# Low parts of the split weights: a GpSimd subtract in SBUF in place of two matmuls and a PSUM copy

## The chip, the cores and the metric

The kernel runs on one core of a Trainium2 chip. A core has five engines that matter here: PE (TensorE, matmuls; PEld is its weight loading), DVE (VectorE), ACT (ScalarE), POOL (GpSimd) and SP (SyncE, which here only issues DMAs). The metric is the device time of one execution in microseconds (us), lower is better. Before the change it was 708.12 us in the median of 3 runs (707.08 to 708.73). One more execution was taken by the hardware profiler; all rows shown come from that one.

## The reference

For each of 4 batches and 8 heads a recurrence with a complex, elementwise decay runs over 768 tokens; its real part is read out by q. The result (3072 tokens x 384) goes through a gated feed-forward layer with weights of 384 x 1536, 384 x 1536 and 1536 x 384:

```python
for t in range(S):
    ar, ai = (a_re_n[:, :, t, :, None], a_im_n[:, :, t, :, None])
    new_re = ar * S_re - ai * S_im
    new_im = ar * S_im + ai * S_re
    kv = np.einsum('bhd,bhe->bhde', k[:, :, t], v[:, :, t])
    S_re, S_im = (new_re + kv, new_im)
    y[:, :, t] = np.einsum('bhd,bhde->bhe', q[:, :, t], S_re)
...
a = x @ w_a
b = x @ w_b
return (a * b @ w_out).astype(np.float32)
```

## The kernel before

**Units.** The work is cut into 12 units u (`NU`): two pairs of batches times six chunks of 128 tokens. Each unit passes through four steps.

- `prep(u)` (mostly DVE, some ACT) forms running products of the decay over the tokens of the chunk (lines 226 and 232 inside sub-blocks, 253 and 259 between them, 274 and 279 to join them), their inverse (282 to 305), and multiplies q and k by them (309 and 294). Line 294 is its last operation. `scale(u)` (177 to 192) works out the normalisation of the decay; that of unit u+1 is woven into `prep(u)`.
- `stack(u)` lays the scaled q and k out by heads with ten DMAs on SP's queue (line 331), from tile `qk` to tile `stk`. There is one `qk` and one `stk`, so the steps of neighbouring units follow each other through them.
- `attn(u)` (PE with DVE and ACT) makes scores from `stk` (364), masks them on DVE (367), transposes the keys (375, 379), multiplies by v and by the carried state (404), and updates the state (421 to 432). Its output is split into a high part `xh`, rounded to fp32r (408, ACT), and a low part `xl` (413, DVE).
- The feed-forward of the unit runs over 12 slices f of the hidden dimension. `gemm1` multiplies in three fp32r passes, high by high, high by low and low by high (465, 18 matmuls for a slice), then forms a*b and splits it again (473 to 476, ACT and DVE in turn). `gemm2` (483) does the same into the output, three slices later.

**Weights.** They arrive as float64 bit patterns: 36 tiles of 128 x 384 (12 slices f, three matrices m), loaded once, at the start. `split_weights` turns each into two fp32r tiles that stay in SBUF for the whole run. For each tile DVE builds the float32 number `t` from the bits with three operations (133, 135, 137); ACT rounds it to the high part `hi` (141); then the low part t - hi is made on PE: an fp32 matmul of `t` with the identity (146, shown as two instructions), plus an fp32r matmul of `hi` with the negative identity (147), both into one PSUM bank, and ACT copies the sum to `lo` (148). The PSUM tile is `ab` for f below 7 and `pm` from there on; these are also the tiles of `gemm1` and of the attention. The float32 `t` lives in tile `o_sb`, of which there are 3 buffers, shared with the output rows.

**Order.** The program text gives `scale(0)`, `prep(0)`, `stack(0)`, then the conversion of six slices, `attn(0)` interleaved with `prep(1)`, and then the loop over units. In unit 0 (w = 0) each slice f first converts one more slice of weights while there are any, `prep(1)` is drained by f = 4 and `stack(1)` issued, and `attn(1)` follows in pieces. The final order on each engine is drawn up when the program is built, by a planner that takes for each engine the earliest instruction in program order that its own cost estimates call ready (raised by `high_priority` for the attention's and the feed-forward's small operations). On the chip each engine then works through its queue in that fixed order. So conversions stand on DVE between the operations of `prep(0)`, where the planner saw gaps, and `attn(1)` ended up behind all of unit 0's feed-forward.

GpSimd does the mask, the identity and three `memset`s at the start (lines 89 to 110) and nothing later.

Of the kernel before, what the change touches and what calls it, by code (L numbers as in the profile page):

```python
# [8 lines left out]
F32 = mybir.dt.float32  # L9
# [5 lines left out]
ALU = mybir.AluOpType  # L15
# [31 lines left out]
CONV_ON_AB = 7  # L47
# [19 lines left out]
def tile_kernel(ctx: ExitStack, tc: tile.TileContext, a_d, qk_d, v_d, w_d, qn_d, kn_d, vn_d, an_d, out_d):  # L67
    nc = tc.nc
    vec, act, pe, sync = nc.vector, nc.scalar, nc.tensor, nc.sync
# [10 lines left out]
    ps_ab = fast.enter_context(tc.tile_pool(name="ps_ab", bufs=3, space=PSUM))  # L80
    ps_o = fast.enter_context(tc.tile_pool(name="ps_o", bufs=1, space=PSUM))
    ps_x = fast.enter_context(tc.tile_pool(name="ps_x", bufs=1, space=PSUM))
    ps_m = fast.enter_context(tc.tile_pool(name="ps_m", bufs=2, space=PSUM))


    ident = const.tile([128, 128], F32, name="ident")
# [26 lines left out]
    nident = const.tile([128, 128], F32, name="nident")  # L113
# [4 lines left out]
    def r(ap):  # L118
        return ap.bitcast(F32R)
# [7 lines left out]
    def split_weights():  # L127
        for f in range(NF):
            for m, (c0, n) in enumerate(WPART):
                raw = raws[f, m]  # L130
                t = moe.tile([128, n], F32, name="o_sb", bufs=O_BUFS)
                tu = t.bitcast(U32)
                vec.tensor_scalar(out=tu, in0=raw[:, :, 1], scalar1=3, scalar2=0x3FFFFFFF,
                                  op0=ALU.logical_shift_left, op1=ALU.bitwise_and)
                vec.scalar_tensor_tensor(out=tu, in0=raw[:, :, 0], scalar=29, in1=tu,
                                         op0=ALU.logical_shift_right, op1=ALU.bitwise_or)
                vec.scalar_tensor_tensor(out=tu, in0=raw[:, :, 1], scalar=0xC0000000, in1=tu,  # L137
                                         op0=ALU.bitwise_and, op1=ALU.bitwise_or)
                w_t[f, m] = wpool.tile([128, 2, n], F32, name=f"w{m}{f}")
                hi, lo = w_t[f, m][:, 0], w_t[f, m][:, 1]  # L140
                act.copy(out=r(hi), in_=t)
                if f < CONV_ON_AB:
                    lp = ps_ab.tile([128, 512], F32, name="ab")
                else:
                    lp = ps_m.tile([128, 512], F32, name="pm")
                pe.matmul(out=lp[:, 0:n], lhsT=ident, rhs=t, start=True, stop=False)  # L146
                pe.matmul(out=lp[:, 0:n], lhsT=r(nident), rhs=r(hi), start=False, stop=True)
                act.copy(out=r(lo), in_=lp[:, 0:n])
            yield


# [440 lines left out]
    def drain(gen, ns=None):  # L592
# [3 lines left out]
        for cost in gen:  # L596
            if left is not None:
                left -= cost or 0
                if left <= 0:
                    return  # L600

    ws = split_weights()
    drain(scale(0, a_tiles[0], z_first))
    drain(prep(0))
# [134 lines left out]
```

## Time and profile before

| quantity | value |
|---|---|
| runs, median (lowest to highest) | 708.12 us (707.08 to 708.73) |
| profiled execution, span from first to last instruction | 708.4 us |
| PE busy | 658.3 us, 93% |
| DVE busy | 565.0 us, 80% |
| ACT busy | 309.6 us, 44% |
| POOL busy | 5.6 us, 1% |
| mean granted TensorE clock | 0.977 |
| core's HBM traffic | 39.32 MB read, 4.72 MB written |

The span of the profiled execution lies inside the range of the three runs, so its microseconds can be set against their median as they are. Busy shares are averages over the whole span; the kernel has a start, in which the weights are converted and the first units are prepared, a long middle in which one unit follows another, and an end without `prep`. The prediction therefore reads the profile in stretches of time, and shows the rows it uses.

In a row of a group of instructions stand: line, engine, operation, tile written <- tiles read, shape, count | busy us, mean ns of one | idle time of the engine just before them and what ended it. In a row of the timeline: start, duration, engine, line, operation, and in brackets the idle time before it. In a row of stretches: busy us of each engine (instructions), granted TensorE clock, DMA share, GB/s.

### The profile page before, as it was taken

Reading aid. Unit: us, or ns where it says so; the run is one execution under the profiler, and the core shown is the slowest. Engines: PE = TensorE matmul, PEld = TensorE weight load, DVE = VectorE, ACT = ScalarE, POOL = GpSimd, SP = SyncE. Lnnn points to the kernel's source line nnn. Section 1 sums busy time; section 2 is a strip of 40 time slices with the busy share of each in tenths; the row PEclk is TensorE's granted clock in tenths of the full one; section 3 lists DMA queues with packets and bytes.
Section 4 is the critical chain, followed back from the end, with each engine's and each line's share of the span. In section 5 each row is a group of like instructions: output and inputs, shape, how many; then the busy total and the mean of one; then the engine's idle time right before and its main releaser. Section 6 shows DMA issues by size and latency. Waiting matters only on the chain.

```text
span 708.4 us, 14429 instructions
## 1 busy us (share of the span) xinstructions
PE 658.3 (93%) x5838; PEld 608.8 (86%) x5838; DVE 565.0 (80%) x1411; ACT 309.6 (44%) x618; POOL 5.6 (1%) x11
## 2 busy tenths in 40 slices
PE   3657899799999999999999999999999999999996
PEld 1224788689899899899899999999999999999995
DVE  5999799888888988888889989999899898332221
ACT  6347565524524624525446346254462424221221
POOL 3000000000000000000000000000000000000000
PEclk9985999989999999999999999999999999999999
DMA  8963300420511512413305125042160140400000
GB/s 316 402 246 90 119 1 1 146 87 1 158 52 41 162 31 68 134 31 106 111 16 157 60 69 149 27 133 74 34 198 2 40 148 12 110 23 2 23 1 28
DMA packets 30234, 63.95 MB, mean 90 GB/s; under 512 B 3664, under 2 KB 7248, under 8 KB 30160
## 3 DMA queue, kind: packets, MB, share of 16 engines
q1 hardware_dynamic: 26704, 58.23, 26.1%
q10 hardware_dynamic: 3456, 4.72, 1.9%
q8 instruction: 48, 0.79, 0.4%
q14 instruction: 26, 0.21, 0.1%
HBM read 39.32 MB, written 4.72 MB: 62 GB/s over the span
## 4 chain that ended last, share of the span: by engine, by line
PE 48%; DVE 37%; ACT 5%; DMA 5%; issue 2%; SPq 1%; DVEq 0%; ACTq 0%
PE ab L465 21%; PE o L483 10%; PE xp L404 6%; PE pm L364 4%; DVE qk L294 4%; DVE a_t L274 4%; DVE pr L226 4%; PE pm L421 3%; DMA stk<-qk 3%; DVE hl L476 3%; DVE h_t L474 3%; DVE z L232 2%; PE pm L375 2%; DVE z L279 2%; DVE pb L253 2%
## 5 line engine op out<-in xcount | busy, mean ns | idle before, releaser
L465 PE MATMUL ab<-xh,w 128*128 128x256 f32 x1728 | 334.5, 283 | 0.0
L465 PEld LDWEIGHTS ab<-xh,w 128*128 128x128 f32 x1728 | 275.5, 189 | 1.7 <-issue 1.0
L465 PE MATMUL ab<-xl,w 128*128 128x256 f32 x864 | 243.6, 282 | 0.0
L465 PEld LDWEIGHTS ab<-xl,w 128*128 128x128 f32 x864 | 162.5, 188 | 1.2 <-issue 0.8
L483 PE MATMUL o<-w,hh 128*128 128x384 f32 x576 | 151.3, 343 | 0.0
L473 ACT COPY h_t<-ab 128x256 f32<-128x256 f32 x144 | 53.3, 370 | 183.1 <-PE ab L465 183.0
L474 DVE TENSOR_TENSOR h_t<-ab,h_t 128x256 f32<-128x256 f32 x144 | 60.5, 420 | 62.2 <-ACT h_t L473 61.7
L483 PEld LDWEIGHTS o<-w,hh 128*128 128x128 f32 x576 | 96.2, 188 | 2.8 <-issue 2.8
L483 PE MATMUL o<-w,hl 128*128 128x384 f32 x288 | 97.3, 338 | 0.0
L475 ACT CAST hh<-h_t 128x256 fp32r<-128x256 f32 x144 | 58.0, 402 | 79.2 <-DVE h_t L474 78.8
L476 DVE TENSOR_TENSOR hl<-h_t,hh 128x256 fp32r<-128x256 f32 x144 | 60.4, 419 | 16.1 <-ACT hh L475 16.1
L364 PE MATMUL pm<-stk 128*128 128x128 f32 x384 | 60.7, 291 | 10.1 <-DMA stk<-qk 9.3
L226 DVE TENSOR_TENSOR pr<-z 128x192 f32<-128x192 f32 (+1 forms) x195 | 65.1, 340 | 5.4 <-ACT z L212 1.6
L364 PEld LDWEIGHTS pm<-stk 128*128 128x128 f32 x384 | 52.3, 199 | 16.4 <-issue 9.9
L146 PE MATMUL ab<-o_sb,ident 128*128 128x384 f32 x42 | 30.8, 835 | 27.8 <-DVE o_sb L137 27.8
L483 PEld LDWEIGHTS o<-w,hl 128*128 128x128 f32 x288 | 54.1, 188 | 0.1
L232 DVE TENSOR_TENSOR z<-pr 128x96 f32<-128x96 f32 (+1 forms) x195 | 47.1, 248 | 3.9
L404 PE MATMUL xp<-am,v_t 128*32 128x128 f32 x768 | 45.2, 283 | 2.7 <-DVE am L367 2.7
L274 DVE TENSOR_TENSOR a_t<-z,b_t 128x768 f32<-128x768 f32 x48 | 45.1, 951 | 0.0
L146 PEld LDWEIGHTS ab<-o_sb,ident 128*128 128x128 f32 x42 | 10.8, 298 | 37.8 <-DVE o_sb L137 27.3
L294 DVE TENSOR_TENSOR qk<-qk,z 128x1536 f32<-128x1536 f32 (+1 forms) x26 | 42.3, 1628 | 0.1
L367 DVE TENSOR_TENSOR am<-pm,mask 128x512 f32<-128x512 f32 x48 | 32.9, 685 | 6.0 <-PE pm L364 5.8
(98 smaller groups left out, 746.5 us busy)
## 6 DMA issues: line engine op xcount, KB each, us to landing
w<-in_dram SPq DMA_DIRECT2D x36, 384.0 KB, 8.0
qk<-in_dram SPq DMA_DIRECT2D x12, 768.0 KB, 4.8
stk<-qk SPq DMA_DIRECT2D x48, 192.0 KB, 3.3
a_t<-in_dram SPq DMA_DIRECT2D x11, 768.0 KB, 4.3
v_t<-in_dram SPq DMA_DIRECT2D x24, 256.0 KB, 2.6
stk<-qk SPq DMA_DIRECT2D x24, 192.8 KB, 3.3
out_dram<-o_sb ACTq DMA_DIRECT2D x24, 192.0 KB, 2.3
stk<-qk SPq DMA_DIRECT2D x16, 128.0 KB, 3.2
```

Source lines behind the costliest of these rows:

```text
L226: vec.tensor_tensor(out=pr[:, :, :, o:o + n], in0=view(zz, W + at_(i) + 2 * o, [[W, 2], [-W, 2], [2, n]]), in1=tok(slice(1, 3), i - 1, o, ...
L232: vec.tensor_tensor(out=tok(slice(1, 3), i, o, n), in0=pr[:, :, 0, o:o + n], in1=pr[:, :, 1, o:o + n], op=ALU.add)
L274: vec.tensor_tensor(out=pz[:, s].rearrange("p (j b e) -> p j b e", j=SUB // 2, e=2), in0=zb[:, 1 + s], in1=view(bb, (1 + k - s) * NB, [[0, ...
L294: vec.tensor_tensor(out=qk4[:, :, k, x0:x1], in0=qk4[:, :, 1, x0:x1], in1=z[:, k].rearrange("p (j t) -> p j t", j=NJ).unsqueeze(2).broadca ...
L364: pe.matmul(out=sp[:, h4], lhsT=stk[:, h, ks], rhs=stk[:, h, qs], start=True, stop=True)
L404: pe.matmul(out=xp[qd * 32:(qd + 1) * 32, ti], lhsT=l, rhs=rr, start=st, stop=sp_, tile_position=(0, qd * 32), skip_group_check=True)
L465: pe.matmul(out=ab[:, m * TOK:(m + 1) * TOK], lhsT=r(w_ab(f, part, m * NJ + i)), rhs=r(xt[:, i, :]), start=n == 0, stop=n == 8)
L473: act.copy(out=h_t, in_=ab[:, 0:TOK])
L474: vec.tensor_tensor(out=h_t, in0=ab[:, TOK:2 * TOK], in1=h_t, op=ALU.mult)
L475: act.copy(out=r(hh), in_=h_t)
L476: vec.tensor_tensor(out=r(hl), in0=h_t, in1=hh, op=ALU.subtract)
L483: pe.matmul(out=os_[tt][:, 0:DM], lhsT=r(ht[:, ts]), rhs=r(w_t[f, 2][:, part, :]), start=(f == 0 and n == 0), stop=(f == NF - 1 and n == 2))
```

## The change

In `split_weights` the PSUM tile, both matmuls and the ACT copy go. The low part is the difference of the same two SBUF tiles, `t` and `hi`, formed by one GpSimd `tensor_tensor` that writes `lo` as fp32r. DVE's three operations and ACT's rounding to `hi` stay. It does this for all 36 tiles.

```diff
                 hi, lo = w_t[f, m][:, 0], w_t[f, m][:, 1]
                 act.copy(out=r(hi), in_=t)
-                if f < CONV_ON_AB:
-                    lp = ps_ab.tile([128, 512], F32, name="ab")
-                else:
-                    lp = ps_m.tile([128, 512], F32, name="pm")
-                pe.matmul(out=lp[:, 0:n], lhsT=ident, rhs=t, start=True, stop=False)
-                pe.matmul(out=lp[:, 0:n], lhsT=r(nident), rhs=r(hi), start=False, stop=True)
-                act.copy(out=r(lo), in_=lp[:, 0:n])
+                nc.gpsimd.tensor_tensor(out=r(lo), in0=t, in1=hi, op=ALU.subtract)
```

## Prediction, made before the run

> **What bounds the kernel now.** I read the slices of the span first, since the edit touches only the weight conversion.
>
> ```profile
> PE 658.3 (93%) x5838; PEld 608.8 (86%) x5838; DVE 565.0 (80%) x1411; ACT 309.6 (44%) x618; POOL 5.6 (1%) x11
> ...
> PE   3657899799999999999999999999999999999996
> ...
> DVE  5999799888888988888889989999899898332221
> ```
>
> By the averages PE is the bound, and taking matmuls off it should pay. By the slices it is different at the start: PE runs at 3 to 7 tenths there and DVE at 9. Stretches of my own, cut where the chain of waits changes hands, say how long that lasts.
>
> ```profile
> core 0: us, PE busy (x) PEld busy (x) DVE busy (x) ACT busy (x) POOL busy (x), PEclk, DMA share, GB/s
> 8.50:61.20 52.70, 33.18 (x57) 14.92 (x57) 51.98 (x163) 26.69 (x53) 0.00 (x0) 0.87 0.74 288
> 61.20:84.00 22.80, 18.48 (x160) 14.81 (x161) 18.55 (x35) 13.90 (x26) 0.00 (x0) 0.78 0.49 151
> 84.00:133.00 49.00, 48.99 (x319) 43.72 (x319) 46.26 (x124) 29.14 (x64) 0.00 (x0) 1.00 0.07 22
> 133.00:157.00 24.00, 19.30 (x218) 15.41 (x217) 19.38 (x46) 11.07 (x17) 0.00 (x0) 0.86 0.43 128
> 157.00:708.00 551.00, 538.30 (x5091) 519.97 (x5090) 427.43 (x1037) 223.73 (x451) 0.00 (x0) 1.00 0.24 71
> ```
>
> From 8.5 us to 61.2 us DVE is busy for 51.98 of 52.70 us; that is `prep(0)` with conversions between its operations. Then comes `attn(0)`, and from 84 to 133 us both engines are full: PE with unit 0's feed-forward and the last conversions, DVE with `prep(1)`, conversions and the feed-forward's small operations. Which of the two decides is told by the chain of waits and by PE's timeline at the end of that stretch.
>
> ```profile
> 129.28 1.67 DVE qk L294
> 131.29 0.51 DVE qk L294
> 131.79 1.07 issue
> ...
> 135.68 4.23 DMA stk<-qk
> 139.95 0.81 PE pm L364 x2
> ```
>
> ```profile
> 134.14 0.34 PE L483 MATMUL o<-w,hl 128*128 128x384 f32 x1
> 136.40 1.01 PE L364 MATMUL pm<-stk 128*128 128x128 f32 x4 [1.92 <-DMA stk<-qk]
> ```
>
> PE ends unit 0's last `gemm2` at 134.48 us and has nothing left: unit 1's feed-forward needs `attn(1)`, which needs `stack(1)`, which needs line 294 of `prep(1)`, the last link on DVE. So up to 133 us DVE's queue sets the time, all 36 conversions included, and PE waits for it even now. After 157 us PE is busy for 538.30 of 551 us. A shift of the moment at which `attn(1)` can start is therefore handed on to the end almost whole, in either direction.
>
> **What is removed.** On PE, before 61.2 us the conversions run beside a saturated DVE and are worth nothing. In the feed-forward stretch there are 15 tiles (those on `pm`):
>
> ```profile
> 85.11 0.81 PE L146 MATMUL pm<-o_sb,ident 128*128 128x384 f32 x2
> 85.46 0.63 PE L147 MATMUL pm<-w,nident 128*128 128x384 f32 x1
> 85.93 0.81 PE L146 MATMUL pm<-o_sb,ident 128*128 128x384 f32 x2
> ```
>
> ```profile
> L147 PE MATMUL pm<-w,nident 128*128 128x384 f32 x15 | 8.0, 541 | 0.0
> L148 ACT CAST w<-ab 128x384 fp32r<-128x384 f32 x21 | 10.0, 477 | 18.3 <-PE ab L147 18.3
> L148 ACT CAST w<-pm 128x384 fp32r<-128x384 f32 x15 | 7.1, 478 | 3.0 <-PE pm L147 3.0
> ```
>
> From one tile's start to the next is 0.82 us, so 15 x 0.82 = 12.3 us of full-speed PE time goes. PE would finish unit 0 near 122 us instead of 134.5 and wait that much longer for `stk`, if DVE ends `prep(1)` when it does now. I count these 12.3 us at nothing; DVE is the cover, and it would have to finish 12 us sooner for all of them to count. ACT loses 10.0 + 7.1 = 17.1 us of copies; at 29.14 of 49 us it bounds no stretch, so that is nothing as well.
>
> What DVE itself can gain is idle time. It idles for 124.5 - (51.98 + 18.55 + 46.26) = 7.7 us between 8.5 and 133 us, and its longest waits are these:
>
> ```profile
> DVE h_t L474 <- ACT h_t L473: 1.6, 2, 0.9
> DVE pr L226 <- ACT z L212: 1.4, 2, 1.0
> DVE o_sb L133 <- DMA w<-in_dram: 1.4, 1, 1.4
> ...
> DVE o_sb L133 <- ACT w L141: 0.6, 1, 0.6
> ```
>
> The first shrinks when `gemm1` isn't delayed by conversions. The others stem from `prep`, a load and ACT; but three float32 tiles converted by 71 us now keep their `o_sb` buffers until PE reaches line 146 at 85.11, so the planner can move up to three tiles' DVE work into gaps between 71 and 85 us. I take -3 us for all of this (1.6 for the feed-forward's wait, the rest for the gaps), between 0 and -5.
>
> **What is added.** 36 subtracts on GpSimd. No row of before shows one. The nearest are its own operations at the start:
>
> ```profile
> L110 POOL MEMSET u<- 128x512 f32 x2 | 1.0, 520 | 0.1
> L90 POOL TENSOR_SCALAR_AFFINE_SELECT mask<-mask 128x128 f32<-128x128 f32 x1 | 0.3, 292 | 0.0
> L89 POOL MEMSET mask<- 128x128 f32 x1 | 0.2, 204 | 0.0
> ```
>
> The two sizes of `memset`, with no input, give (520 - 204) / 384 = 0.82 ns per element and 0.10 us fixed. The select reads one input: (292 - 99) / 128 = 1.51 ns per element, so an input adds 0.69. With two inputs that is 2.20 ns per element, and a 128 x 384 subtract takes 0.10 + 0.84 = 0.94 us. The lower bound is the memset's 0.42 us. The Trainium skill, "GPSIMD Engine Reference", section 3.1, gives 4497 ns for a two-input operation on 2048 elements; scaled to 384 that is an estimate of 0.84 us, which would make the sum below some 3 us smaller; no run so far shows one.
>
> As a queue, GpSimd carries this easily: nothing else is in it after 6.3 us, and 36 x 0.94 = 34 us lie in a stretch of 125. Behind a waiting subtract stand only later subtracts. Those who wait for it are `gemm1` and `gemm2` of its slice, and DVE's line 133 three tiles later, through the `o_sb` buffer. That loop is DVE 1.2 us, ACT 0.5 and GpSimd 0.94, near 2.7 us with three buffers, 0.9 us a tile; DVE needs 1.2 us of its own for one. Not a bound.
>
> What can cost is DVE itself. Its operations in these stretches, by kind:
>
> ```profile
> L135 DVE SCALAR_TENSOR_TENSOR o_sb<-w,o_sb 128x384 uint32<-128x384 uint32 x36 | 19.8, 552 | 0.1
> L137 DVE SCALAR_TENSOR_TENSOR o_sb<-w,o_sb 128x384 uint32<-128x384 uint32 x36 | 19.8, 552 | 0.1
> L133 DVE TENSOR_SCALAR o_sb<-w 128x384 uint32<-128x384 uint32 x36 | 12.7, 354 | 2.1 <-DMA w<-in_dram 1.4 <-ACT w L141 0.6
> ...
> L474 DVE TENSOR_TENSOR h_t<-ab,h_t 128x256 f32<-128x256 f32 x12 | 5.1, 421 | 1.6 <-ACT h_t L473 1.6
> ...
> L367 DVE TENSOR_TENSOR am<-pm,mask 128x512 f32<-128x512 f32 x4 | 2.8, 688 | 0.8 <-PE pm L364 0.8
> ...
> L413 DVE TENSOR_TENSOR xl<-xp,xh 128x384 fp32r<-128x384 f32 x2 | 1.1, 558 | 0.9 <-ACT xh L408 0.9
> ```
>
> Nearly all of DVE's work here reads two SBUF operands. For the same 384 elements line 133, with one operand, takes 354 ns and line 135, with two, 552 ns: supplying the second operand is what DVE's time goes into. A subtract on GpSimd reads two SBUF operands too. If both are served by the same reader, one stands while the other works. The trace has one overlap:
>
> ```profile
> 5.36 0.98 POOL L110 MEMSET u<- 128x512 f32 x2
> 5.49 0.56 DVE L178 SCALAR_TENSOR_TENSOR z<-z 128x384 f32<-128x384 f32 x1 [4.34 <-ACT z L177]
> ...
> 6.61 0.56 DVE L178 SCALAR_TENSOR_TENSOR z<-z 128x384 f32<-128x384 f32 x1 [0.57 <-ACT z L177]
> ```
>
> Line 178 takes 0.56 us beside GpSimd and 0.56 us without. But the memset reads nothing, so this excludes only a hold by writes. The price per subtract lies between 0 and 0.94 us of DVE time. I take a full hold whenever DVE is at a two-operand operation, because line 135 against 133 is the nearest row for what a second SBUF operand costs, and the memset row is of another kind. That share is 116.8 us busy, less 12.7 (133), 5.1 (474), 2.8 (367), 1.1 (413) and about 1.2 of small ones, so 93.9 of 124.5 us, or 0.75. The sum is 36 x 0.94 x 0.75 = +25.5 us.
>
> The Trainium skill, "SBUF — State Buffer" (its practical consequences of the port allocation), speaks against this change in so many words: DVE with two SBUF inputs and GpSimd reading SBUF share a read interface, and the later one fully blocks. By that rule the whole +25.5 us would be due; no run so far shows it.
>
> One more term is PE's clock.
>
> ```profile
> 64.00:66.00 2.00, 2.00 (x6) 1.24 (x5) 1.88 (x6) 1.24 (x3) 0.00 (x0) 0.50 0.81 233
> ...
> 68.00:70.00 2.00, 1.37 (x21) 0.98 (x20) 2.00 (x4) 1.48 (x4) 0.00 (x0) 1.00 0.73 197
> ```
>
> The granted clock is 0.50 as `attn(0)` starts and 1.00 from 68 us; the conversion matmuls keep PE busy just before. Without them `attn(0)` may run at 0.50 for some microseconds more. PE has gaps there, so I count 0, at most +3.
>
> **Sum.** 708.4 + 25.5 - 3 = 730.9, taken as 731 us. The span of 708.4 lies 0.3 us from the runs' median of 708.12, which changes nothing. With every subtract held against DVE whole (+33.8) and no gain it is 742; with no hold and the full -5 it is 703. A measurement of this kernel can tell about 0.2%, or 1.4 us, from no change.
>
> **Rivals.** *GpSimd works beside DVE.* If its reads do not stand in DVE's way, 708.4 - 3 gives 705 us, faster by 0.5%; the place is again the end of `prep(1)` on DVE. For it: GpSimd is idle, and the one overlap in the trace costs nothing. Against: that overlap reads nothing. It turns slower once a subtract costs DVE more than 3 / 36 = 0.08 us. Chance 0.17.
>
> *Half a hold.* If the operands interleave, or the planner puts many subtracts where DVE waits or reads PSUM, half of 25.5 less 3 gives +10, or 718 us. Chance 0.16.
>
> *PE's time counts.* If conversions on PE delay DVE through `h_t` more than I see, the 12.3 us come back: 696 us. For it: between 93 and 108 us the chain of waits runs over PE. Against: DVE still idles for only 2.7 us of the 49, so it cannot end much sooner. Chance 0.03.
>
> *More than a hold.* If writing fp32r or handing over between engines makes a subtract cost above 0.94 us, each 0.3 us more gives 36 x 0.3 x 0.75 = 8 us: 739 to 750. Chance 0.10.
>
> **How the numbers follow.** The forecast, a hold of some 0.5 to 0.9 us of DVE time per subtract, has 0.54; its own range is 722 to 742. Faster: 0.13 of the first rival's 0.17 and the 0.03, so 0.16. Within 0.2%: the rest of the first rival and an edge of the half hold, 0.05. Slower: 0.79. The range from 703 to 743 leaves out the 696 case and most of the last rival.
>
> **What would show it.** Right: POOL busy near 34 us in some 36 subtracts; DVE's line 135 and the scan operations at lines 226 and 232 longer in the mean, or gaps before them with a POOL releaser or none; the first line 364 after `stack(0)` later by 10 to 18 us than 64.8, `stack(1)` later by 20 or more than 133; PE idle long before `attn(1)`; from there on the stretches as long as now. Wrong: DVE's rows keep their durations (then 705), or `stack(1)` moves forward by more than 5 us.

## The result, and the profile after

| | median (lowest to highest), us | runs |
|---|---|---|
| before | 708.01 (707.08 to 708.73) | 4 |
| after | 732.35 (731.14 to 733.48) | 4 |

The change makes the kernel slower: ratio 1.034, 95% interval 1.0319 to 1.0361, +24.3 us. The profiled execution after has a span of 729.9 us and belongs to a run of 731.64 us. In the later runs, too, a span lies 1.7 to 2.1 us under its run's time, so the 708.4 us span of before belongs to an execution some 2 us above the median. The two traces therefore differ by 21.5 us where the medians differ by 24.3.

In the changed kernel every line behind 142 has a number lower by 6: 226 is 220, 259 is 253, 294 is 288, 331 is 325, 364 is 358, 474 is 468. Its page begins like this (engines, then the slices):

```profile
PE 615.1 (84%) x5730; PEld 589.9 (81%) x5730; DVE 590.5 (81%) x1411; ACT 295.7 (41%) x582; POOL 58.2 (8%) x47
...
PE   0000599719999999999999999999999999999997
...
DVE  6999889978898888888998989999899999323221
...
POOL 5344214300000000000000000000000000000000
```

PE has lost its 36 conversions (108 instructions) and does nothing in the first four slices. DVE has as many instructions as before (1411) and is busy for 25.5 us more. That is the whole result in one line: work that DVE was not given takes DVE time. The stretches, cut where those of before were cut (start, `stack(0)`, `stack(1)`, some 24 us later):

```profile
core 0: us, PE busy (x) PEld busy (x) DVE busy (x) ACT busy (x) POOL busy (x), PEclk, DMA share, GB/s
7.10:73.25 66.15, 0.00 (x0) 0.00 (x0) 65.68 (x163) 20.43 (x38) 29.05 (x19) 1.00 0.61 236
73.25:159.90 86.65, 61.04 (x432) 56.67 (x432) 77.62 (x160) 36.29 (x73) 23.57 (x18) 0.89 0.19 56
159.90:184.00 24.10, 19.49 (x223) 16.46 (x224) 21.32 (x55) 10.44 (x15) 0.00 (x0) 0.75 0.43 117
184.00:730.00 546.00, 534.58 (x5077) 516.80 (x5075) 424.61 (x1026) 224.87 (x451) 0.00 (x0) 1.00 0.24 72
```

Up to `stack(1)` the stretch was 124.5 us with DVE busy for 116.8 us; now it is 66.15 + 86.65 = 152.8 us with DVE busy for 65.68 + 77.62 = 143.3 us. So DVE's work grew by 26.5 us and its idle time from 7.7 to 9.5 us. The end of that stretch, in the chain of waits (start, us, engine, tile and line):

```profile
138.75 1.13 POOL w L142
139.93 1.86 PE ab L459 x7
141.79 5.13 PE o L477 x21
146.99 0.49 ACT o_sb L616
147.98 0.49 ACT o_sb L616
148.88 1.49 ACT a_t L276
...
158.09 1.77 DVE qk L288
159.88 0.59 SPq L325
...
162.63 3.09 DMA stk<-qk
165.77 0.81 PE pm L358 x2
```

`stack(1)`'s DMAs are issued at 159.88 us; on SP's timeline of before it was 132.98 us. That is 26.9 us later, 12.0 of it already at `stack(0)` (73.25 against 61.22). From there to the end after needs 570.0 us and before 575.4, so 5.4 us come back. 26.9 - 5.4 gives the 21.5 us between the spans. (Executions differ by a little here: e10 below, whose program up to unit 10 is that of before, issues `stack(1)` at 130.30 us. The shift is 27 to 30 us.)

How the hold looks in one place, on the timeline around 67 us:

```profile
66.23 1.10 POOL L142 TENSOR_TENSOR w<-o_sb,w 128x384 fp32r<-128x384 f32 x1 [1.04 <-ACT w L141]
66.40 1.34 DVE L137 SCALAR_TENSOR_TENSOR o_sb<-w,o_sb 128x384 uint32<-128x384 uint32 x1
67.67 0.94 DVE L299 SCALAR_TENSOR_TENSOR a_t<-a_t 128x768 f32<-128x768 f32 x1
...
68.36 1.10 POOL L142 TENSOR_TENSOR w<-o_sb,w 128x384 fp32r<-128x384 f32 x1 [1.04 <-ACT w L141]
68.53 1.14 DVE L133 TENSOR_SCALAR o_sb<-w 128x384 uint32<-128x384 uint32 x1
```

Line 137 took 0.55 us before and takes 1.34 here; line 133 took 0.35 and takes 1.14. Both carry the same 0.79 us more, whatever their own length. That reads as follows: the DVE instruction that comes up while a subtract runs stands until that has nearly ended, and then takes its usual time. It counts as busy meanwhile, so the hold shows in no list of waits. It shows when each DVE instruction is set against others of its line and shape (their lower quartile): up to `stack(1)` exactly 36 are longer by over 0.15 us, for 36 subtracts, 26 of them by 0.79 to 0.85 us, 26.2 us in all. The same comparison gives none for before. In the groups (up to 160 us):

```profile
L137 DVE SCALAR_TENSOR_TENSOR o_sb<-w,o_sb 128x384 uint32<-128x384 uint32 x36 | 22.1, 616 | 0.1
L135 DVE SCALAR_TENSOR_TENSOR o_sb<-w,o_sb 128x384 uint32<-128x384 uint32 x36 | 21.9, 612 | 0.1
L133 DVE TENSOR_SCALAR o_sb<-w 128x384 uint32<-128x384 uint32 x36 | 15.0, 422 | 0.0
L253 DVE TENSOR_TENSOR b_t<-pb 128x12 f32<-128x12 f32 x15 | 7.4, 496 | 0.0
L468 DVE TENSOR_TENSOR h_t<-ab,h_t 128x256 f32<-128x256 f32 x12 | 4.9, 412 | 0.0
L361 DVE TENSOR_TENSOR am<-pm,mask 128x512 f32<-128x512 f32 x4 | 2.8, 688 | 2.4 <-PE pm L358 2.4
```

Lines 135 and 137 rose from 552 ns, 133 from 354. Line 253, a tiny operation, went from 175 ns (line 259 before) to 496: six of its 15 were held. Lines 468 and 361, which read one of their operands from PSUM, stayed at their 421 and 688 ns. They ran beside a working subtract in four places only, and in none of them are they longer. One of the four:

```profile
123.74 1.43 POOL L142 TENSOR_TENSOR w<-o_sb,w 128x384 fp32r<-128x384 f32 x1 [2.01 <-ACT w L141]
123.75 0.55 DVE L135 SCALAR_TENSOR_TENSOR o_sb<-w,o_sb 128x384 uint32<-128x384 uint32 x1
...
124.22 0.41 DVE L468 TENSOR_TENSOR h_t<-ab,h_t 128x256 f32<-128x256 f32 x1
...
124.55 0.84 DVE L220 TENSOR_TENSOR pr<-z 128x192 f32<-128x192 f32 x1
```

Line 468 passes in its usual 0.41 us, and line 220 behind it (0.35 us by itself) carries what is left of the hold, 0.48 us.

### The profile page after: what moved, and what is told of

The parts are those of the page before. It is cut to its first block, busy times and chain, and to the rows that moved or that the text cites. A ratio compares the mean times of both kernels' runs of the same rounds, so it can differ in the third digit from the quotient of the medians.

```text
span 729.9 us, 14256 instructions
## 1 busy us (share of the span) xinstructions
PE 615.1 (84%) x5730; PEld 589.9 (81%) x5730; DVE 590.5 (81%) x1411; ACT 295.7 (41%) x582; POOL 58.2 (8%) x47
## 4 chain that ended last, share of the span: by engine, by line
PE 45%; DVE 41%; ACT 4%; issue 4%; DMA 3%; SPq 1%; POOL 0%; ACTq 0%; DVEq 0%; POOLq 0%
PE ab L459 20%; PE o L477 10%; PE xp L398 5%; DVE pr L220 5%; PE pm L358 5%; DVE a_t L268 4%; DVE qk L288 3%; DVE h_t L468 3%; DVE z L226 3%; DMA stk<-qk 3%; PE pm L415 3%; DVE hl L470 3%; DVE b_t L253 2%; DVE o_sb L135 2%; DVE pb L247 2%
## 5 line engine op out<-in xcount | busy, mean ns | idle before, releaser
L477 PE MATMUL o<-w,hh 128*128 128x384 f32 x576 | 153.0, 346 | 0.0
L358 PE MATMUL pm<-stk 128*128 128x128 f32 x384 | 64.2, 303 | 98.5 <-DMA stk<-qk 98.2
L358 PEld LDWEIGHTS pm<-stk 128*128 128x128 f32 x384 | 54.8, 207 | 104.6 <-issue 101.0
L477 PEld LDWEIGHTS o<-w,hh 128*128 128x128 f32 x576 | 97.8, 191 | 2.8 <-issue 2.6
L470 DVE TENSOR_TENSOR hl<-h_t,hh 128x256 fp32r<-128x256 f32 x144 | 62.0, 431 | 16.8 <-ACT hh L469 16.5
L220 DVE TENSOR_TENSOR pr<-z 128x192 f32<-128x192 f32 (+1 forms) x195 | 70.1, 366 | 4.7 <-ACT z L206 0.6
L142 POOL TENSOR_TENSOR w<-o_sb,w 128x384 fp32r<-128x384 f32 x36 | 52.6, 1470 | 82.0 <-ACT w L141 65.5
L141 ACT CAST w<-o_sb 128x384 fp32r<-128x384 f32 x36 | 18.3, 510 | 55.9 <-DVE o_sb L137 52.7
```

What stands on the lines that cost most here:

```text
L220: vec.tensor_tensor(out=pr[:, :, :, o:o + n], in0=view(zz, W + at_(i) + 2 * o, [[W, 2], [-W, 2], [2, n]]), in1=tok(slice(1, 3), i - 1, o, ...
L358: pe.matmul(out=sp[:, h4], lhsT=stk[:, h, ks], rhs=stk[:, h, qs], start=True, stop=True)
L470: vec.tensor_tensor(out=r(hl), in0=h_t, in1=hh, op=ALU.subtract)
L477: pe.matmul(out=os_[tt][:, 0:DM], lhsT=r(ht[:, ts]), rhs=r(w_t[f, 2][:, part, :]), start=(f == 0 and n == 0), stop=(f == NF - 1 and n == 2))
```

## The experiments

Each kernel ran on one chip beside the kernel before, and its ratio is against those runs. `stack(0)` and `stack(1)` are the times at which SP issues their DMAs, from each kernel's trace; "held" is the comparison just described, in instructions and us.

| kernel | median us | ratio to before, 95% | stack(0) | stack(1) | held |
|---|---|---|---|---|---|
| after | 732.35 | 1.034 (1.0319 to 1.0361) | 73.25 | 159.88 | 36, 26.2 us |
| e1_memset | 703.87 | 0.9945 (0.9923 to 0.9967) | 59.99 | 133.75 | 3, 0.9 us |
| e2_dve | 719.95 | 1.0175 (1.0158 to 1.0192) | 61.31 | 140.41 | none |
| e3_both | 738.86 | 1.045 (1.0424 to 1.0475) | 75.75 | 161.22 | 31, 23.4 us |
| e4_twice | 757.68 | 1.071 (1.0692 to 1.0729) | 89.05 | 184.31 | 69, 52.7 us |
| e5_copy | 713.20 | 1.0074 (1.0046 to 1.0103) | 65.40 | 139.38 | 27, 7.8 us |
| e6_late | 716.37 | 1.0117 (1.0088 to 1.0146) | 60.37 | 143.00 | 14, 10.0 us |
| e7_early | 724.44 | 1.022 (1.0188 to 1.0252) | 74.35 | 149.38 | 21, 16.1 us |
| e8_prio | 707.49 | 0.9993 (0.9975 to 1.001) | 60.52 | 131.87 | none |
| e10_tail | 707.22 | 0.9989 (0.9977 to 1.0001) | 59.75 | 130.30 | none |
| e11_act | 705.23 | 0.9964 (0.995 to 0.9978) | 59.94 | 131.02 | none |

The theory is the prediction's: GpSimd's reads of SBUF hold DVE. The rivals are that any occupied GpSimd does it, that the loss lies in the path of the low part (GpSimd's own length, buffers, order), or that the missing PE and ACT work plays a part.

**A GpSimd instruction that reads nothing.**

```diff
-                nc.gpsimd.tensor_tensor(out=r(lo), in0=t, in1=hi, op=ALU.subtract)
+                nc.gpsimd.memset(lo.bitcast(U32), 0)
```

> The subtract is replaced by a GpSimd memset of lo, which reads nothing; the low parts of the weights are left out (zero). If DVE lost its time to a hold by GpSimd's reads: DVE's rows keep their durations of before (line 135 at 0.55 us, 226 at 0.25), and with the matmuls and copies gone as in the change the time is 705 us (702 to 709). If the change lost its time to a new order of the planner, to buffers released later or to a cold PE clock: 720 to 732. If GpSimd's writes hold DVE as well: 718 to 725.

Groups of e1, up to 190 us:

```profile
L137 DVE SCALAR_TENSOR_TENSOR o_sb<-w,o_sb 128x384 uint32<-128x384 uint32 x36 | 19.8, 552 | 0.0
L135 DVE SCALAR_TENSOR_TENSOR o_sb<-w,o_sb 128x384 uint32<-128x384 uint32 x36 | 19.8, 552 | 0.1
...
L142 POOL MEMSET w<- 128x384 uint32 x36 | 15.1, 418 | 93.1 <-DVE o_sb L137 93.0
...
L133 DVE TENSOR_SCALAR o_sb<-w 128x384 uint32<-128x384 uint32 x36 | 13.5, 377 | 0.2 <-DMA w<-in_dram 0.2
```

36 GpSimd instructions in the same place of the program, and lines 135 and 137 keep their 552 ns to the nanosecond. The kernel is 4.0 us faster than before. An occupied GpSimd is thus hardly a cost; what a subtract adds to a memset is. One exception shows on e1's timeline:

```profile
100.36 0.42 POOL L142 MEMSET w<- 128x384 uint32 x1 [7.86 <-DVE o_sb L137]
100.38 0.61 DVE L133 TENSOR_SCALAR o_sb<-w 128x384 uint32<-128x384 uint32 x1
```

Three instructions of line 133, which has one operand, ran beside a whole memset (this one, and two at 8.87 and 83.83 us), and they are longer by 0.25 to 0.34 us. So a GpSimd instruction that only writes leaves the two-operand lines alone, but not line 133.

**One input, two inputs, two subtracts.** e5 puts a copy in the subtract's place, e4 issues the subtract twice:

```diff
-                nc.gpsimd.tensor_tensor(out=r(lo), in0=t, in1=hi, op=ALU.subtract)
+                nc.gpsimd.tensor_copy(out=r(lo), in_=t)
```

> GpSimd copies t into lo, one SBUF input in place of two (lo then holds t, so the difference is left out). If any GpSimd read holds DVE's two-operand instructions: a shorter hold, about 0.4 to 0.5 us each, 715 to 721 us, and single DVE rows longer by that much. If only an instruction with two inputs holds DVE: 703 to 706 us as with the memset.

> The change with every subtract done twice (same operands, same result). If each subtract holds DVE by about 0.70 us: another 25 us, 752 to 760 us. If the loss has another cause and GpSimd works beside DVE: 732 to 736 us.

The timeline of e5, a copy beside line 226:

```profile
29.03 0.64 POOL L142 CAST w<-o_sb 128x384 fp32r<-128x384 f32 x1 [2.61 <-DVE o_sb L137]
29.22 0.62 DVE L226 TENSOR_TENSOR z<-pr 128x48 f32<-128x48 f32 x2
...
30.37 0.32 DVE L226 TENSOR_TENSOR z<-pr 128x48 f32<-128x48 f32 x2
```

The copy costs DVE 0.62 - 0.32 = 0.30 us; of 27 held instructions 20 show 0.30 to 0.32. That is less than the 0.4 to 0.5 us expected, and so is the loss (713.20 us against 715 to 721). So on two-operand lines the hold grows with what GpSimd reads: none for the memset, 0.31 us for one input, 0.80 us for two. e4's groups, up to 190 us:

```profile
L142 POOL TENSOR_TENSOR w<-o_sb,w 128x384 fp32r<-128x384 f32 x36 | 45.3, 1258 | 68.9 <-ACT w L141 68.9
L143 POOL TENSOR_TENSOR w<-o_sb,w 128x384 fp32r<-128x384 f32 x36 | 43.9, 1221 | 2.7
```

72 subtracts hold 69 DVE instructions for 52.7 us, twice the 26.2, and the kernel is 25.3 us slower than after. Among the four kernels without PE's part and with GpSimd instead (e1, e5, after, e4) the time rises from 703.87 to 757.68 us while the held time rises from 0.9 to 52.7 us: 53.8 us for 51.8. DVE's hold is handed on almost one for one.

**The subtract on DVE itself.**

```diff
-                nc.gpsimd.tensor_tensor(out=r(lo), in0=t, in1=hi, op=ALU.subtract)
+                vec.tensor_tensor(out=r(lo), in0=t, in1=hi, op=ALU.subtract)
```

> The same subtract, done by DVE itself (36 x 0.47 us = 17 us more in its queue). If a GpSimd subtract costs DVE about 0.70 us each, doing it on DVE is cheaper: stack(1) 17 to 19 us later than before, 720 to 724 us in all. If GpSimd's subtract took little from DVE, this is the dearest version: 732 us or more.

The group of that line, up to 190 us:

```profile
L142 DVE TENSOR_TENSOR w<-o_sb,w 128x384 fp32r<-128x384 f32 x36 | 19.7, 552 | 0.0
```

DVE does the subtract in 0.55 us, and the kernel is 12.4 us faster than after. A subtract on GpSimd takes more of DVE's time (26.2 us for 36, 0.73 each) than the same subtract on DVE. There is a second effect: only 15 tiles stand ahead of `stack(0)` here and 2 behind `stack(1)`; before and after have 19 and none. `stack(0)` keeps its place (61.31 us), and `stack(1)` comes 7.4 us later than in before's trace, where 17 to 19 were expected. That reads as the planner reckoning with the price of a DVE instruction and spreading the work, while the hold is not in its costs: after's order has the tiles where before's has them.

**The subtract added to the kernel before.** e3 issues the subtract into `lo` and then lets PE and ACT write the same values as before:

```diff
                 act.copy(out=r(hi), in_=t)
+                nc.gpsimd.tensor_tensor(out=r(lo), in0=t, in1=hi, op=ALU.subtract)
```

> The kernel before with both matmuls and the PSUM copy kept, and the GpSimd subtract added in front of them (the copy then writes lo again). If the subtract alone costs the time: 729 to 735 us, as much as the change. If the removal of the matmuls costs it (PE clock, new order): 708 to 712 us. If the removal is worth its 12 us of PE time and the hold costs more than it seems: 740 us or more.

With PE and ACT doing all that they did, the time still rises, by 31.0 us: the loss does not come from what was taken away. That is between the two outcomes expected (729 to 735, and 740 or more). 23.4 us of it are held DVE instructions. Where the rest comes from isn't shown; one candidate is a wait that this edit makes itself, seen in e3's groups up to 190 us (the old ACT copy is its line 149):

```profile
L149 ACT CAST w<-ab 128x384 fp32r<-128x384 f32 x21 | 9.9, 477 | 27.7 <-PE ab L148 15.0 <-POOL w L142 12.7
```

**Half of the tiles.** e6 uses the subtract for f of 7 and up (15 tiles), e7 for f below 7 (21 tiles); the others go over PE and ACT:

```diff
                 act.copy(out=r(hi), in_=t)
+                if f >= CONV_ON_AB:
+                    nc.gpsimd.tensor_tensor(out=r(lo), in0=t, in1=hi, op=ALU.subtract)
+                    continue
```

> GpSimd subtracts the 15 tiles from f = 7 on; PE and ACT keep the first 21. If the hold is 0.70 us a tile and the removal is worth 4 to 6 us, all of it here where PE is full: 10.5 less 5, 711 to 716 us. If the late tiles cost nothing because PE is what counts there: 696 to 704 us.

> The other part: GpSimd subtracts the first 21 tiles, PE and ACT keep the last 15. The hold is 21 x 0.70 = 15 us and nothing is won on PE, which idles there: 720 to 726 us. If the early stretch has slack (loads, waits on ACT): 708 to 712 us.

Against the 708.65 us of before on the same chip they are 7.7 and 15.8 us slower, together 23.5, where the whole change is 24.3. Per tile that is 0.51 and 0.75 us. e7 lies in the range expected of a hold, e6 just above its own. Each half is worse than leaving its tiles on PE, so neither of the two divisions tried gains, and nothing in them points to one that would. In the 15 late tiles, which free 12 us of full-speed PE time, the loss is the smaller of the two, but it is a loss.

**Is PE's or ACT's part worth anything?** e8 leaves the computation as it was and raises the priority of the matmuls and the ACT copy:

```diff
+                with tc.high_priority(offset=MOE_FIRST):
                     pe.matmul(out=lp[:, 0:n], lhsT=ident, rhs=t, start=True, stop=False)
...
                     act.copy(out=r(lo), in_=lp[:, 0:n])
```

> The kernel before, with the two matmuls and the copy of each conversion raised in the planner's order, so that PE frees the float32 buffers earlier and DVE can convert in its gaps from 71 to 85 us. If the 4 us that the memset version gains come from those buffers and from the feed-forward's waits: 704 to 707 us. If they come from PE's or ACT's time itself: 707 to 709 us, no change.

e11 takes PE and GpSimd out altogether and lets ACT write `lo`:

```diff
-                nc.gpsimd.tensor_tensor(out=r(lo), in0=t, in1=hi, op=ALU.subtract)
+                act.copy(out=r(lo), in_=t)
```

> The matmuls go and neither GpSimd nor DVE gets the work: ACT copies t into lo (the difference is left out, lo holds t), one ACT copy a tile as before. If the 4 us of the memset version come from PE's 15 late tiles and the PSUM tiles they held: 703 to 705 us. If they come from ACT's 17 us: 707 to 709 us.

The priority changes nothing that can be measured (ratio 0.9993, interval 0.9975 to 1.001). Without PE's conversions and without a hold the kernel gains 2.9 us in e11 and 4.0 us in e1. That is about what all of PE's 36 conversions are worth. In e1 PE ends unit 0's last `gemm2` at 120.9 us instead of 134.5 and then stands; PE's waits between 60 and 170 us in e1:

```profile
PE pm L358 <- DMA stk<-qk: 80.2, 3, 63.5
```

63.5 us of that is the wait for `stack(0)` and most of the rest the one for `stack(1)`.

**GpSimd where DVE is not the bound.** Could a subtract on GpSimd pay elsewhere? e10 moves the feed-forward's split (line 476) of the last two units, where DVE's slices show two to three tenths, to GpSimd:

```diff
-    def gemm1(f, xh, xl, ps_ab=ps_ab, moe=moe):
+    def gemm1(f, xh, xl, ps_ab=ps_ab, moe=moe, sub=vec):
...
-            vec.tensor_tensor(out=r(hl), in0=h_t, in1=hh, op=ALU.subtract)
+            sub.tensor_tensor(out=r(hl), in0=h_t, in1=hh, op=ALU.subtract)
...
-            pend.append((w, f, *gemm1(f, *x_cur), os_))
+            pend.append((w, f, *gemm1(f, *x_cur, sub=nc.gpsimd if w >= NU - 2 else vec), os_))
```

> A control in the place where DVE does not decide: the kernel before, with the 24 low parts hl of the last two units (128 x 256 each) subtracted by GpSimd in place of DVE. If GpSimd's subtracts cost only through DVE's queue where that queue sets the time: 706.5 to 709.5 us, no change, with DVE rows held here as well. If a GpSimd subtract slows the kernel by itself (its latency, its port): 24 x 0.5 to 0.7, 718 us or more.

Its GpSimd group after 600 us, and one overlap on its timeline:

```profile
L476 POOL TENSOR_TENSOR hl<-h_t,hh 128x256 fp32r<-128x256 f32 x24 | 17.8, 743 | 672.6 <-ACT hh L475 672.6
```

```profile
640.72 0.69 DVE L367 TENSOR_TENSOR am<-pm,mask 128x512 f32<-128x512 f32 x1
...
641.23 0.74 POOL L476 TENSOR_TENSOR hl<-h_t,hh 128x256 fp32r<-128x256 f32 x1 [6.24 <-ACT hh L475]
```

Where a hold was expected here too, none came. That says little of the hold: DVE does nothing at all beside 20 of the 24 subtracts. The other four meet four instructions of line 367 and one of line 413, all with one operand in PSUM, and all five keep their usual length (0.69 and 0.56 us). The subtract is slower than DVE's 424 ns by 0.32 us, and the kernel comes out no different from before (0.9989, interval 0.9977 to 1.0001).

## Why the prediction was right

It said 731 us, by a hold of DVE; the median is 732.35 us, and the hold is what the runs show. The mechanism was right. That the number came out within 1.4 us is partly luck: two errors in the hold cancel, the gain of 3 us came from another place than the one named, and `stack(1)` moved by 27 to 30 us, more than the 22.5 of the sum, of which 5.4 came back. Step by step:

**DVE's queue up to `stack(1)` sets the time.** Right. Held DVE time is handed on nearly one for one (e1, e5, after, e4). That a shift of `stack(1)` reaches the end "almost whole" holds with a correction: 5.4 of 26.9 us came back. From `stack(1)` to the end after, e1, e4, e5 and e6 need 569.1 to 571.4 us, and before, e2, e3, e7, e8 and e11 need 572.3 to 575.5. One part of it can be seen: `stk`'s last transfer on the chain takes 3.09 us now and took 4.23 before, when unit 0's output left beside it. It is not PE's matmuls alone, since e11 has none either and needs 573.0. e6, which does without PE and ACT in the 15 late tiles alone, is in the first group, and e7, which keeps them there, is in the second. With e11, which keeps ACT's copies, that points to those copies; only e2 does not fit, and it converts two tiles behind `stack(1)`. Whether it is the ACT copies or the order in which units 1 and 2 are laid out stays open.

**The hold, 36 x 0.94 x 0.75 = 25.5 us.** The sum is right (26.2), and by luck, since its factors were wrong in opposite ways. One subtract, at 78.18 us, found no DVE instruction running: it takes 1.00 us, not 0.94, and holds DVE for 0.85. Each of the other 35 ends 0.85 to 0.88 us after a DVE instruction with all operands in SBUF that went ahead of it, and holds the next one mostly for 0.80. So part of a subtract's span is its own waiting, and the price per hit was below the 0.94. And the share is not 0.75: all 36 struck something. The share left line 133 out because it reads one operand; but it is held like the others (1.14 us against 0.35), as is line 231, another `tensor_scalar`. Only the operations with an operand in PSUM were right to leave out. Besides, a DVE that is at such an operation is soon at the next one. Now and then the hit is partial (ten of the 36 are under 0.79, four of them behind line 468 or 361), which makes the mean 0.73. The Trainium skill, "SBUF — State Buffer", section "Who interferes with whom", lists `tensor_scalar` among the operations that can take both ports and then contend with GpSimd; the trace agrees in that both lines are held, though it doesn't show which ports they used. The same section says that an operation with one SBUF input outside those modes doesn't contend, and that a GpSimd instruction which only writes doesn't disturb DVE's two inputs; lines 468 and 361 and e1's lines 135 and 137 agree. Its wording that the loser blocks for the whole instruction is a little more than the runs show: 0.85 of 1.00 us at 78.18.

The prediction took its full hold from lines 133 and 135: 354 against 552 ns for the same 384 elements, read as the price of a second SBUF operand. Before's groups don't bear that reading out. Line 226 takes 354 ns for 192 elements and line 135 552 for 384, both with two SBUF operands, which is 1.03 ns for each further element; line 367, with only one operand in SBUF, needs 688 ns for 512 and so the same. Line 133 is the one that differs: with 186 ns for the 48 elements of line 237 and 354 for its 384 a `tensor_scalar` takes 0.50 ns for each further element, twice the pace. The conclusion from the pair was right, the reason was not.

**POOL busy near 34 us.** Wrong: 52.6 us for the 36, 1470 ns each in the mean. The prediction had DVE held by GpSimd and not the reverse. On after's timeline:

```profile
55.57 1.81 DVE L268 TENSOR_TENSOR a_t<-z,b_t 128x768 f32<-128x768 f32 x2
...
56.27 5.31 POOL L142 TENSOR_TENSOR w<-o_sb,w 128x384 fp32r<-128x384 f32 x1 [3.49 <-ACT w L141]
57.31 0.95 DVE L288 TENSOR_TENSOR qk<-qk,z 128x768 f32<-128x768 f32 x1
...
59.05 0.35 DVE L133 TENSOR_SCALAR o_sb<-w 128x384 uint32<-128x384 uint32 x1
```

The subtract stands for 5.31 us behind a train of DVE operations without a gap. Being held is cheap for GpSimd, as the prediction's buffer loop has it, except at the very end (below).

**The gain of 3 us from DVE's idle time.** Right in size, wrong in place. Without a hold the removal gives 2.9 to 4.0 us (e11, e1); but DVE's idle time ahead of `stack(1)` did not shrink, it grew from 7.7 to 9.5 us. In e1 `stack(1)` comes 0.8 us later than in before's trace, so its gain lies wholly behind it. Why the idle grew is on the chain and on DVE's timeline:

```profile
146.97 0.93 DVE L273 TENSOR_TENSOR z<-a_t 128x768 f32<-128x768 f32 x1
...
148.88 1.48 ACT L276 ACTIVATE a_t<-z 128x1536 f32<-128x1536 f32 x1 [0.42 <-ACT o_sb L616]
150.39 0.96 DVE L282 TENSOR_TENSOR a_t<-a_t 128x768 f32<-128x768 f32 x1 [2.36 <-ACT a_t L276]
...
153.32 0.96 DVE L297 TENSOR_TENSOR a_t<-a_t 128x768 f32<-128x768 f32 x1 [1.97 <-ACT a_t L284]
```

DVE waits 2.36 and 1.97 us there; before it was 0.62 and 0.41 at the same operations. PE is done with unit 0 by 147 us, so no small feed-forward operations are left to fill DVE's pauses (before, lines 474 and 476 ran in them), and ACT reaches line 276 only behind the two output copies of line 616, which wait for the last `gemm2` and so for the last two subtracts.

**PE's 12.3 us and ACT's 17.1 us at nothing.** Nearly right: without PE's conversions e1 and e11 gain 2.9 to 4.0 us, and e1's PE finishes unit 0 early and then waits. The rival of 696 us is excluded; the best kernel without conversions is at 703.87.

**The span as the base.** The prediction set the span of 708.4 us against the median as if both measured the same. A run's time lies some 1.75 us above its span, so the base was an execution about 2 us slow. It moves the forecast by about 2 us, less than the terms above.

**PE's clock, 0 to +3 us, counted 0.** Right at `attn(0)`: between 76 and 96 us the granted clock is 1.00, against 0.50 and 0.55 before at the same work. It was not quite nothing at the end of unit 0. There PE waits for the last weights, and from 140 to 144 us the clock is 0.50, where before had 1.00 from 84 to 138 us. The first of the 21 matmuls of `gemm2` on the chain start every 0.32 us, the last ones, with the clock back, every 0.17. Line 276 starts at 148.88 us behind them, while its input from line 273 was there at 147.90, so the clock can have cost at most some 1 us of `stack(1)`, inside the range given. Around `attn(1)` the clock is lower than before (0.75 in the third stretch, against 0.86), but the time from `stack(1)` on is shorter, so no loss is to be seen.

**The rivals.** Without a hold (705) is what e1 and e11 are, and their 703.87 and 705.23 confirm that sum. Half a hold (718) and more than a hold (739 and up) are out: the comparison counts 36 hits of mostly 0.8 us.

## What to carry to other kernels

In these runs work given to an idle GpSimd was free for DVE only if it read nothing from SBUF (and even then line 133 lost 0.25 to 0.34 us beside it), or if what DVE did meanwhile took an operand from PSUM; otherwise an instruction on 128 x 384 elements took 0.3 us (one input) or 0.8 us (two) from DVE, and DVE does the whole subtract itself in 0.55 us. Such a hold is in no list of waits: compare the durations of one line's instructions in the two traces, and count the long ones against the other engine's instructions. And before work is taken off the engine with the largest busy share, look which engine's queue ends last in that stretch: taking away all of PE's 36 conversions was worth 3 to 4 us of 708.

## What was not expected of the hardware

Three things. The hold has a size of its own: operations of 128 x 12 and of 128 x 384 elements both carried 0.8 us, and it is a little shorter than the GpSimd instruction that causes it (0.31 us for a copy, of which the shortest took 0.50; 0.80 to 0.85 for a subtract, of which the shortest took 1.00). DVE's one-operand `tensor_scalar` meets it as well, and even beside a memset, by 0.25 to 0.34 us. And it works in both directions, with up to 5.31 us for one subtract.
